# Swapped products first, and more of x and v loaded before the first period, in a long-convolution and MLP kernel

## The chip, the cores and the metric

The kernel runs on one core of a Trainium2 chip. The metric is the time of one execution on the device in microseconds (us).

## The reference

A long convolution by FFT, gated by x on both sides, and an MLP on its result:

```
h_filt = (max(pos_emb @ w1, 0) @ w2) * exp(-0.01 * pos)      # (12480, 128)
u      = x * v                                               # (4, 12480, 128)
y      = irfft(rfft(u, 2S) * rfft(h_filt, 2S))[:, :S]        # S = 12480
x2     = (x * y).reshape(49920, 128)
h      = x2 @ w_in                                           # (49920, 2048)
out    = (h * clip(h + 3, 0, 6) / 6) @ w_out                 # (49920, 128)
```

All in 32-bit floats.

## The kernel before, in words

The order of the instructions on each engine is that of the code. Transfers are all issued on SP's queue, in the code's order, and a transfer into a buffer waits there until the buffer's last reader is done.

The convolution is a Fourier transform in two stages each way. It comes in 8 *groups* of 32 channels and 2 batch rows. For a group: a product u = x * v on POOL (a *gate*, L453, in *halves* of 16 channels: 8 halves a group), a first stage on PE (L282, copied to the tile z by ACT, L294), a second stage (L301) that makes the spectrum, the product with the filter's spectrum h (`products`), a third stage (L546, copied by ACT, L550), then transposes (L557, copied by ACT, L560) and a fourth stage (L575, results L594 and L596).

`filter` runs first. It makes the filter's spectrum, and in its last part does group 0's first stage: 8 *visits* of 4 first-stage steps. Then come 8 *periods*, one a group. `period(g)` goes through 25 *chunks* of 4 frequencies: products of chunk c, third stage of an earlier chunk, second stage of chunk c + 1. Between chunks it does the transposes of group g - 1, the visits of group g + 1 and the decoding of the MLP's weights on DVE (`weight`, L225 to L247, and L243 on ACT). So the second stage of chunk c + 1 goes into one of two banks in PSUM (`s2`), which chunk c - 1 used, and waits until all readers of that bank are done. In `products`, ACT copies the spectrum into a bank `sw` (one buffer) with halves swapped and one negated (L499, L500, "the swap"). DVE makes four products, "the block": q and a from the spectrum's bank (L520, L521), q2 and a2 from the swapped bank (L522, L523). POOL adds them up (L527). In period 0 the last addition of two chunks in three is on DVE (L533).

x and v come in halves into the pool xv (two buffers). During the filter three more halves go into a pool ext. `gate_next` multiplies the next loaded half, and if its buffers were of xv, loads a further half into them. A list of chunks in `period` says when (GATES, and GATES0 for period 0).

After the periods the MLP runs (class Moe, from about 1000 us to the end). The change doesn't touch it.

Of the kernel before, what the change touches and what calls it, by code (L numbers as in the profile page):

```python
# [38 lines left out]
GB = 2  # L39
# [24 lines left out]
VISIT = 4  # L64
GATES = (1, 4, 8, 11, 14, 17, 20, 22)
GATES0 = (0, 2, 4, 8, 11, 14, 17, 20, 22)
NT = 8
NH = 4

# [119 lines left out]
def pool(tc, name, bufs=1, **kw):  # L189
    return tc.tile_pool(name=name, bufs=bufs, reuse_waits="tile", **kw)  # L190
# [60 lines left out]
class Conv:  # L251
# [54 lines left out]
    def filter(self, pos_emb, w1, w2, f_tab, win_d, ident_d):  # L306
        tc, nc = self.tc, self.nc
# [64 lines left out]
        def spectrum(half, c, stp):  # L372

            t, kw = self.second_stage(ftab[:, c * CH :], z, c)
            tv = t.rearrange("p (k s g c) -> p k s g c", k=CH, s=2, c=G)
            st = stp.tile([P, 2, CH, 2, G], F32, tag="st", name="st")
            sv = st.rearrange("p g k s c -> p k s g c")
            nc.scalar.copy(sv[:, :kw, 0], tv[:, :kw, 0])
            for i, op in ((0, ALU.add), (1, ALU.subtract)):
                nc.vector.tensor_tensor(out=sv[:, i:kw:2, 1], in0=tv[:, i:kw:2, 1], in1=sv[:, i:kw:2, 0], op=op)  # L380
            nc.sync.dma_start(
                self.hd[half].rearrange("g p k s c -> p g k (s c)")[:, :, c * CH : c * CH + kw],
                st[:, :, :kw].rearrange("p g k s c -> p g k (s c)"),
            )
# [12 lines left out]
            spectrum(0, c, st0)  # L397
        early.close()
        self.ext = ExitStack()
        ext = self.ext.enter_context(pool(tc, "ext", 3, side="right"))  # L400
        for piece in range(2 * GB):
            for j in range(G // 4):
                self.first_stage(z, u[:, piece], 0, piece, j)
# [2 lines left out]
        large.close()  # L406
        self.ft = self.left.enter_context(pool(tc, "ft", NT))
        st1 = large.enter_context(pool(tc, "st1", 12))
        for c in range(NCHUNK):
            spectrum(1, c, st1)  # L410
            if c % 2 and self.n_tabs < NT:
                self.load_tab()
        large.close()
        left, right = self.left, self.right
# [31 lines left out]
    def gate_next(self):  # L446

        if self.loaded:
            half, xt, vt, again = self.loaded.pop(0)
            if half == 0:  # L450
                self.gated.append(self.up.tile([R[0], G, N1], F32, tag="u", name="u"))
            u = self.gated[-1][:, half * G // 2 : (half + 1) * G // 2, :]
            self.nc.gpsimd.tensor_tensor(out=u, in0=xt, in1=vt, op=ALU.mult)  # L453
            if again:
                self.load_next()

    def visit(self, g, m):

        piece, j = divmod(m * VISIT, G // 4)
        for i in range(VISIT):  # L460
            self.first_stage(self.z[g % 2], self.gated[0], piece // GB, piece, j + i)
        if j + VISIT == G // 4:
            self.gated.pop(0)
# [39 lines left out]
    def products(self, item):  # L503

        nc, P = self.nc, 128
        g, c, kw, t, tab = item
        sw = self.swapped(t, kw)
        hs = self.hs.pop(0)
        a = self.pr.tile([P, CH, 2 * GB, G], F32, tag="a", name="pa", bufs=4)
        a2 = self.pr.tile([P, CH, 2 * GB, G], F32, tag="a2", name="pa2")  # L510
        q = self.pr.tile([P, CH, GB, G], F32, tag="q", name="pq")
        q2 = self.pr.tile([P, CH, GB, G], F32, tag="q2", name="pq2")
        uv = t.rearrange("p (k s g) -> p k s g", k=CH, g=G)[:, :kw]
        sv = sw.rearrange("p (k s g) -> p k s g", k=CH, g=G)[:, :kw]

        def h(ci, si, m):
            return hs[:, ci, :kw, si, :].unsqueeze(2).to_broadcast([P, kw, m, G])

        mul, add = ALU.mult, ALU.add
        nc.vector.tensor_tensor(out=q[:, :kw], in0=uv[:, :, :GB], in1=h(0, 1, GB), op=mul)  # L520
        nc.vector.tensor_tensor(out=a[:, :kw], in0=uv, in1=h(0, 0, 2 * GB), op=mul)  # L521
        nc.vector.tensor_tensor(out=q2[:, :kw], in0=sv[:, :, :GB], in1=h(1, 1, GB), op=mul)  # L522
        nc.vector.tensor_tensor(out=a2[:, :kw], in0=sv, in1=h(1, 0, 2 * GB), op=mul)  # L523
        self.load_h()

        def plus(x, y):
            nc.gpsimd.tensor_tensor(out=x, in0=x, in1=y, op=add)  # L527

        plus(a[:, :kw, GB:], q[:, :kw])
        plus(a2[:, :kw, GB:], q2[:, :kw])  # L530
        if self.sum:
            s, s2 = self.sum
            nc.vector.tensor_tensor(out=s, in0=s, in1=s2, op=add)  # L533
        self.sum = None
        if g == 0 and c % 3:
            self.sum = a[:, :kw], a2[:, :kw]
        else:
            plus(a[:, :kw], a2[:, :kw])
        return g, c, kw, tab, a
# [61 lines left out]
    def period(self, g):  # L601


        n = 0
        if g == 1:
            self.ext.close()
            self.dp = self.left.enter_context(pool(self.tc, "dp"))
            self.wp = self.right.enter_context(pool(self.tc, "wp", 2, side="right"))
        for c in range(NCHUNK):
            end = min(32, 32 * (c + 1 - START) // (NCHUNK - 1 - START))  # L610
            self.chunk(g, c)
            if c in (0, NCHUNK - 1):
                self.fourth_stage()
            if c in (GATES if g else GATES0):
                self.gate_next()
            while n < end:
                if g:
                    self.back(g - 1, 4 * n)
                    self.weight(n)
                n += 1  # L620
                if n % VISIT == 0:
                    if g + 1 < NG:
                        self.visit(g + 1, n // VISIT - 1)
                    if n < 28 and g + 1 < NG:
                        self.fourth_stage()
                if n % VISIT == 2 and VISIT < n < 28 and g + 1 == NG:
                    self.fourth_stage()
# [267 lines left out]
```

## Time and profile before

| | |
|---|---|
| time, median of 3 runs | 3170.02 us (3169.38 to 3170.16) |
| the profiled execution: time | 3166.51 us |
| its span, first to last instruction | 3164.7 us |
| PE, ACT, DVE, POOL busy in the span | 98%, 74%, 73%, 66% |
| granted TensorE clock, mean | 0.998 |
| moved by DMA | 304.66 MB |
| waits of L301 for L521 | 27.9 us, 21 times |

A row of the order of time has the start in us from the span's start, the length in us, the engine, the line, the operation, the tiles (out<-in, numbers left out, so that the banks s2, sw and s3 may read s, sw and s), how many instructions were merged, and in brackets how long the engine was idle before and what ended that. PE is TensorE, DVE is VectorE, ACT is ScalarE, POOL is GpSimd. The filter runs until 158 us, period 0 to about 242, and the other periods take some 111 us each. In this text chunk k's L301 is the second stage that makes chunk k's spectrum, and block k its four products.

### The profile page before, as it was taken

To read this page: it belongs to the slowest core of one execution; us is meant where nothing else is said; L and a number is where in the kernel's file an instruction comes from. 1 tells how busy PE (TensorE), PEld (TensorE's weight loads), DVE (VectorE), ACT (ScalarE), POOL (GpSimd) and SP (SyncE) were. 2 spreads that over 40 slices of the span, in tenths; PEclk is the share of its full clock that TensorE was granted. 3 is DMA by queue.
4 is the path that set the end of the run, shared out by engine and by line. 5 is a ranking of instruction groups with operands and counts; after the bars stand their busy time and mean duration, and the time that the engine had idled before them with its cause. 6 is when DMAs were issued, how large, how long until landed. Compare 5 with 4: busy or idle time off the path is not lost.

```text
span 3164.7 us, 53332 instructions
## 1 busy us (share of the span) xinstructions
PE 3114.2 (98%) x19916; PEld 2633.9 (83%) x19916; DVE 2305.8 (73%) x2707; ACT 2351.7 (74%) x3039; POOL 2079.2 (66%) x1240
## 2 busy tenths in 40 slices
PE   9989999999999999999999999999999999999999
PEld 8978888888887788888888888888888888888887
DVE  4467666767654777777777777777777777777776
ACT  2367767767766777878787777777777877777777
POOL 1188777777874666666666666666666666666666
PEclk9999999999999999999999999999999999999999
DMA  6688888787855111111111110111111111111110
GB/s 236 211 205 230 228 230 234 218 238 221 228 172 202 54 36 35 38 42 35 35 40 31 41 41 30 41 39 32 41 36 35 39 32 41 38 33 40 40 31 24
DMA packets 232273, 304.66 MB, mean 96 GB/s; under 512 B 38055, under 2 KB 159310, under 8 KB 231118
## 3 DMA queue, kind: packets, MB, share of 16 engines
q1 hardware_dynamic: 232014, 301.26, 32.6%
q8 instruction: 157, 2.57, 0.3%
q14 instruction: 102, 0.84, 0.1%
HBM read 224.87 MB, written 76.28 MB: 95 GB/s over the span
## 4 chain that ended last, share of the span: by engine, by line
PE 68%; POOL 0%; DVE 0%; ACT 0%; DMA 0%; issue 0%; ACTq 0%
PE acc L827 11%; PE acc L823 11%; PE acc L824 11%; PE ph L788 11%; PE ph L790 11%; PE ph L789 11%; PE ts L575 0%; PE s L557 0%; PE ts L557 0%; POOL pa L527 0%; DMA yd<-y 0%; POOL glo L812 0%; DVE y L596 0%; ACT o L594 0%; ACT ghi L810 0%
## 5 line engine op out<-in xcount | busy, mean ns | idle before, releaser
L812 POOL TENSOR_TENSOR glo<-g,ghi 128x1024 fp32r<-128x1024 f32 x588 | 1404.4, 2397 | 761.2 <-ACT ghi L810 761.0
L800 DVE SCALAR_TENSOR_TENSOR g<-r,ph 128x1024 f32<-128x1024 f32 (+1 forms) x784 | 949.7, 1211 | 408.7 <-ACT r L798 408.3
L798 ACT ACTIVATE r<-ph,three 128x1024 f32<-128x1024 f32 (+1 forms) x784 | 871.1, 1111 | 273.6 <-PE ph L790 273.4
L810 ACT CAST ghi<-g 128x1024 fp32r<-128x1024 f32 (+1 forms) x784 | 811.1, 1035 | 1.9 <-DVE g L800 1.0
L788 PE MATMUL ph<-xhi,win_hi 128*128 128x512 f32 (+1 forms) x1568 | 608.5, 388 | 0.0
L789 PE MATMUL ph<-xlo,win_hi 128*128 128x512 f32 (+1 forms) x1568 | 608.4, 388 | 0.0
L790 PE MATMUL ph<-xhi,win_lo 128*128 128x512 f32 (+1 forms) x1568 | 608.3, 388 | 0.0
L824 PE MATMUL acc<-ghi,wout_lo 128*128 128x512 f32 (+1 forms) x1568 | 608.0, 388 | 0.0
L823 PE MATMUL acc<-ghi,wout_hi 128*128 128x512 f32 (+1 forms) x1568 | 607.9, 388 | 0.0
L827 PE MATMUL acc<-glo,wout_hi 128*128 128x512 f32 (+1 forms) x1568 | 481.3, 388 | 0.6 <-POOL glo L812 0.6
L527 POOL TENSOR_TENSOR pa<-pa,pq 128x256 f32<-128x256 f32 (+1 forms) x400 | 295.6, 747 | 171.3 <-DVE pa L521 133.2
L788 PEld LDWEIGHTS ph<-xhi,win_hi 128*128 128x128 f32 x1568 | 294.4, 188 | 61.5 <-issue 0.8
L827 PEld LDWEIGHTS acc<-glo,wout_hi 128*128 128x128 f32 x1568 | 293.6, 188 | 61.7 <-POOL glo L812 1.5
L824 PEld LDWEIGHTS acc<-ghi,wout_lo 128*128 128x128 f32 x1568 | 294.5, 188 | 60.5
L790 PEld LDWEIGHTS ph<-xhi,win_lo 128*128 128x128 f32 x1568 | 294.4, 188 | 60.5
L823 PEld LDWEIGHTS acc<-ghi,wout_hi 128*128 128x128 f32 x1568 | 294.4, 188 | 60.4
L789 PEld LDWEIGHTS ph<-xlo,win_hi 128*128 128x128 f32 x1568 | 294.5, 188 | 60.4
L812 DVE TENSOR_TENSOR glo<-g,ghi 128x1024 fp32r<-128x1024 f32 x196 | 283.7, 1448 | 0.0
L520 DVE TENSOR_TENSOR pq<-s,h 128x256 f32<-128x256 f32 (+1 forms) x200 | 84.1, 421 | 255.7 <-POOL pa L527 162.2
L761 DVE TENSOR_TENSOR xy<-xt,yt 128x512 f32<-128x512 f32 x96 | 258.7, 2695 | 0.0
L301 PE MATMUL s<-z,tab 128*128 128x128 f32 x1584 | 213.9, 278 | 35.5 <-DVE pa L521 27.9
L527 POOL TENSOR_TENSOR pa<-pa,pa 128x512 f32<-128x512 f32 (+1 forms) x184 | 232.5, 1263 | 14.4
(61 smaller groups left out, 3620.6 us busy)
## 6 DMA issues: line engine op xcount, KB each, us to landing
tab<-in_g_tab SPq DMA_DIRECT2D x192, 256.0 KB
h<-hd SPq DMA_DIRECT2D x384, 128.0 KB
yd<-y SPq DMA_DIRECT2D x64, 512.0 KB
xt<-in_xt SPq DMA_DIRECT2D x98, 256.0 KB
out<-o SPq DMA_DIRECT2D x97, 256.0 KB
xt<-in_x SPq DMA_DIRECT2D x64, 384.0 KB
vt<-in_v SPq DMA_DIRECT2D x64, 384.0 KB
yt<-yd SPq DMA_DIRECT2D x256, 64.0 KB
```

Of the source, the lines that this page charges most:

```text
L527: nc.gpsimd.tensor_tensor(out=x, in0=x, in1=y, op=add)
L761: self.nc.vector.tensor_tensor(out=xy.rearrange("p (n e c) -> p n e c", e=4, c=GH), in0=xt.rearrange("p (n e c) -> p n e c", e=4, c=GH), i ...
L788: nc.tensor.matmul(ph[:, i, :ne], self.win_hi[:, sl], hi[:, :ne], start=True, stop=False)
L789: nc.tensor.matmul(ph[:, i, :ne], self.win_hi[:, sl], lo[:, :ne], start=False, stop=False)
L790: nc.tensor.matmul(ph[:, i, :ne], self.win_lo[:, sl], hi[:, :ne], start=False, stop=True)
L798: nc.scalar.activation(r[:, :, :ne], ph[:, :, :ne], AF.Relu, bias=self.three)
L800: nc.vector.scalar_tensor_tensor(out=g[:, :, :ne], in0=r[:, :, :ne], scalar=6.0, in1=ph[:, :, :ne], op0=ALU.min, op1=ALU.mult)
L810: nc.scalar.copy(ghi[:, :, :ne], g[:, :, :ne])
L812: e.tensor_tensor(out=glo[:, :, :ne], in0=g[:, :, :ne], in1=ghi[:, :, :ne].bitcast(F32), op=ALU.subtract)
L823: nc.tensor.matmul(a, self.wout_hi[:, f, :], ghi[:, i, :ne], start=(f == 0), stop=False)
L824: nc.tensor.matmul(a, self.wout_lo[:, f, :], ghi[:, i, :ne], start=False, stop=False)
L827: nc.tensor.matmul(a, self.wout_hi[:, f, :], glo[:, i, :ne], start=False, stop=(f == NFC - 1))
```

## The change

Three things:

- In `products` q2 and a2, which read the swapped bank, are made before q and a, which read the spectrum's bank. POOL's additions follow in the same order.
- `gate_next`, while it runs in the filter, loads a further half also after a half of the pool ext, into ext again: three halves more are under way before period 0.
- In period 0 the visits of group 1 come at chunks 0, 2, 6, 9, 12, 15, 18 and 21. Before, they came at chunks 3, 6, 9, 12, 15, 18, 21 and 23.

```diff
+VISITS0 = (2, 6, 9, 12, 15, 18, 21)
...
-        ext = self.ext.enter_context(pool(tc, "ext", 3, side="right"))
+        ext = self.spare = self.ext.enter_context(pool(tc, "ext", 3, side="right"))
...
             if again:
                 self.load_next()
+            elif self.ps is None:
+                self.load_next(self.spare)
...
+        nc.vector.tensor_tensor(out=q2[:, :kw], in0=sv[:, :, :GB], in1=h(1, 1, GB), op=mul)
+        nc.vector.tensor_tensor(out=a2[:, :kw], in0=sv, in1=h(1, 0, 2 * GB), op=mul)
         nc.vector.tensor_tensor(out=q[:, :kw], in0=uv[:, :, :GB], in1=h(0, 1, GB), op=mul)
         nc.vector.tensor_tensor(out=a[:, :kw], in0=uv, in1=h(0, 0, 2 * GB), op=mul)
-        nc.vector.tensor_tensor(out=q2[:, :kw], in0=sv[:, :, :GB], in1=h(1, 1, GB), op=mul)
-        nc.vector.tensor_tensor(out=a2[:, :kw], in0=sv, in1=h(1, 0, 2 * GB), op=mul)
...
+        plus(a2[:, :kw, GB:], q2[:, :kw])
         plus(a[:, :kw, GB:], q[:, :kw])
-        plus(a2[:, :kw, GB:], q2[:, :kw])
...
             end = min(32, 32 * (c + 1 - START) // (NCHUNK - 1 - START))
+            if g == 0:
+                end = VISIT * (1 + sum(c >= i for i in VISITS0))
```

Line numbers of the changed kernel are a little higher: L520 to L523 are L525, L526, L523 and L524 there, L301 is L302, L282 is L283, L442 is L443, L484 is L487, L546 is L549.

DVE, in period 1, around a block in the weights' decoding (s2 is the spectrum's bank, sw the swapped one, h the filter's spectrum), before:

```order
L241 SCALAR_TENSOR_TENSOR dec_3596<-dec_3596 128x256
L520 TENSOR_TENSOR pq_3916<-s2_3887,h_3690 128x256
L521 TENSOR_TENSOR pa_3914<-s2_3887,h_3690 128x512
L522 TENSOR_TENSOR pq2_3917<-sw_3911,h_3690 128x256
L523 TENSOR_TENSOR pa2_3915<-sw_3911,h_3690 128x512
L245 TENSOR_TENSOR dec_3596<-dec_3596,raw_3594 128x256
```

The same place on DVE now:

```order
L242 SCALAR_TENSOR_TENSOR dec_3596<-dec_3596 128x256
L523 TENSOR_TENSOR pq2_3917<-sw_3911,h_3690 128x256
L524 TENSOR_TENSOR pa2_3915<-sw_3911,h_3690 128x512
L525 TENSOR_TENSOR pq_3916<-s2_3887,h_3690 128x256
L526 TENSOR_TENSOR pa_3914<-s2_3887,h_3690 128x512
L246 TENSOR_TENSOR dec_3596<-dec_3596,raw_3594 128x256
```

The two products of the spectrum's bank (s2_3887) moved from the block's start to its end; what stands around the block stayed.

PE at the start of period 0 (u_1819 is the last piece of group 0, u_1902 and u_1914 the first of group 1; every second stage is an L301 or L302), before:

```order
L301 MATMUL s2_1988<-z0_78,tab_1380 128x128 x4
L301 MATMUL s2_2010<-z0_78,tab_1402 128x128 x4
L301 MATMUL s2_2038<-z0_78,tab_1424 128x128 x4
L301 MATMUL s2_2060<-z0_78,tab_1446 128x128 x4
L546 MATMUL s3_2091<-pa_1996,tab_1380 128x128 x4
L301 MATMUL s2_2099<-z0_78,tab_1468 128x128 x4
L282 MATMUL ts_2104<-ctab_84,u_1902 64x99 x8
```

The same place on PE now:

```order
L302 MATMUL s2_2006<-z0_78,tab_1380 128x128 x4
L302 MATMUL s2_2028<-z0_78,tab_1402 128x128 x4
L283 MATMUL ts_2040<-ctab_84,u_1914 64x99 x8
L283 MATMUL ts_2050<-ctab_84,u_1914 64x99 x8
L283 MATMUL ts_2060<-ctab_84,u_1914 64x99 x8
L283 MATMUL ts_2070<-ctab_84,u_1914 64x99 x8
L302 MATMUL s2_2096<-z0_78,tab_1424 128x128 x4
L302 MATMUL s2_2118<-z0_78,tab_1446 128x128 x4
L283 MATMUL ts_2131<-ctab_84,u_1914 64x99 x8
```

The first visit (four first-stage steps) moved from behind chunk 4's second stage to behind chunk 1's, and the second visit to behind chunk 3's.

SP from the filter's end to the first h load of period 0 (h_1641 is the last h load of the filter; each half is two issues for x and two for v), before:

```order
L484 DMA h_1641<-hd0_57 64x2x256 x2
L442 DMA xt_1726<-in_x 96x1024
L442 DMA xt_1726<-in_x 2x1024
L442 DMA vt_1727<-in_v 96x1024
L442 DMA vt_1727<-in_v 2x1024
L442 DMA xt_1733<-in_x 96x1024
L442 DMA xt_1733<-in_x 2x1024
L442 DMA vt_1734<-in_v 96x1024
L442 DMA vt_1734<-in_v 2x1024
L484 DMA h_2004<-hd0_57 64x2x256 x2
L442 DMA xt_2016<-in_x 96x1024
```

The same place on SP now, from the second issue of the third half on:

```order
L443 DMA xt_1821<-in_x 2x1024
L443 DMA vt_1822<-in_v 96x1024
L443 DMA vt_1822<-in_v 2x1024
L443 DMA xt_1828<-in_x 96x1024
L443 DMA xt_1828<-in_x 2x1024
L443 DMA vt_1829<-in_v 96x1024
L443 DMA vt_1829<-in_v 2x1024
L443 DMA xt_1916<-in_x 96x1024
L443 DMA xt_1916<-in_x 2x1024
L443 DMA vt_1917<-in_v 96x1024
L443 DMA vt_1917<-in_v 2x1024
L487 DMA h_2022<-hd0_57 64x2x256 x2
```

Three halves (xt_1821, xt_1828 and xt_1916, with their v), twelve issues, moved ahead of the first h load.

## The prediction, made before the changed kernel was run

> **What bounds the kernel now.** I read the page's engine shares first, then the waits, then busy time by stretch, then the order of time on PE, ACT and DVE inside one period. From the page, and from the list of waits (total, times, longest, in us):
>
> ```profile
> PE 3114.2 (98%) x19916; PEld 2633.9 (83%) x19916; DVE 2305.8 (73%) x2707; ACT 2351.7 (74%) x3039; POOL 2079.2 (66%) x1240
> ...
> ACT sw L499 <- DVE pa L523: 97.3, 85, 2.6
> POOL u L453 <- DMA vt<-in_v: 39.9, 2, 35.6
> PE s L301 <- DVE pa L521: 27.9, 21, 2.1
> ```
>
> PE is busy 98% of the span, so a gain can only come out of some 50 us of idle PE; whatever makes PE wait costs in full, since it works through its matmuls in order. Its largest wait is that of the second stage (L301) for the product L521, which frees a spectrum bank. ACT's copies into the swapped bank (L499) wait longer in sum, but ACT has room.
>
> Busy time by stretch: us, PE, PEld, DVE, ACT, POOL, clock, DMA share, GB/s.
>
> ```profile
> 158.00:170.00 12.00, 7.62 (x48) 7.21 (x48) 6.89 (x14) 3.81 (x7) 7.54 (x8) 0.86 0.20 58
> 190.60:200.90 10.30, 8.91 (x113) 8.36 (x112) 7.26 (x15) 6.65 (x14) 8.63 (x9) 1.00 0.89 217
> 335.00:339.00 4.00, 3.86 (x36) 3.61 (x38) 3.93 (x7) 2.41 (x5) 3.76 (x4) 0.67 0.58 163
> ```
>
> Period 0 begins at 158 with idle DMAs and goes on in cycles of three chunks, 10.30 us each, in which no engine is full. Later periods are PE's.
>
> **The change: products of the swapped spectrum first.** No instruction is added. In a DVE block of four products, L520 and L521 read the spectrum bank (two of them), L522 and L523 the swapped bank (one). Now the swapped bank comes free two products earlier and the spectrum bank two later. The block starts when the swap is done in either order, as these rows of period 3 show (chunk 4's end to chunk 7's L301):
>
> ```profile
> 485.07 0.84 PE L557 MATMUL ts<-ident,z 128*99 128x128 f32 x4
> 488.21 1.06 PE L546 MATMUL s<-pa,tab 128*128 128x128 f32 x8
> 489.10 1.11 PE L301 MATMUL s<-z,tab 128*128 128x128 f32 x8
> 485.94 0.59 ACT L560 COPY w<-ts 99x512 f32<-99x512 f32 x1 [0.98 <-PE ts L557]
> 486.56 0.56 ACT L499 COPY sw<-s 64x512 f32<-64x512 f32 x1
> 487.14 0.57 ACT L500 ACTIVATE sw<-s 64x512 f32<-64x512 f32 x1
> 487.80 0.42 DVE L520 TENSOR_TENSOR pq<-s,h 128x256 f32<-128x256 f32 x1 [1.33 <-POOL pa L527]
> 488.14 0.68 DVE L521 TENSOR_TENSOR pa<-s,h 128x512 f32<-128x512 f32 x1
> 489.07 0.68 DVE L523 TENSOR_TENSOR pa<-sw,h 128x512 f32<-128x512 f32 x1
> ```
>
> The swap at 486.56 follows ACT's copy L560, which follows PE's L557; the swap ends at 487.71, the block starts 0.09 later. The releaser named for L520 (POOL) is not the last one: the swap is. L521 ends at 488.82, and L301 of chunk 7, which takes the bank that L521 frees, starts 0.28 later, 0.89 after L546: PE is just not late. With the new order the product that frees this bank ends where L523 ends now, 489.75, which is 0.93 later; L301 starts at about 490.03, and PE idles 0.93. The earlier swapped bank can't move this block forward, since its swap waits for PE through L560, not for the bank.
>
> How often is L301 that close? The same period's other pairs, in the order chunk 4 (PE waits already), 10, 16, 19, 21, 22, 24; each L301 with the L521 two blocks before:
>
> ```profile
> 476.16 1.13 PE L301 MATMUL s<-z,tab 128*128 128x128 f32 x8 [0.71 <-DVE pa L521]
> 501.72 0.68 DVE L521 TENSOR_TENSOR pa<-s,h 128x512 f32<-128x512 f32 x1
> 502.71 1.06 PE L301 MATMUL s<-z,tab 128*128 128x128 f32 x8
> 528.33 0.68 DVE L521 TENSOR_TENSOR pa<-s,h 128x512 f32<-128x512 f32 x1
> 529.11 1.13 PE L301 MATMUL s<-z,tab 128*128 128x128 f32 x8 [0.47 <-ACT raw L243]
> 541.11 0.68 DVE L521 TENSOR_TENSOR pa<-s,h 128x512 f32<-128x512 f32 x1
> 542.07 1.06 PE L301 MATMUL s<-z,tab 128*128 128x128 f32 x8
> 551.52 0.68 DVE L521 TENSOR_TENSOR pa<-s,h 128x512 f32<-128x512 f32 x1
> 552.48 1.06 PE L301 MATMUL s<-z,tab 128*128 128x128 f32 x8
> 557.16 1.13 PE L301 MATMUL s<-z,tab 128*128 128x128 f32 x8 [2.06 <-DVE pa L521]
> 566.71 0.68 DVE L521 TENSOR_TENSOR pa<-s,h 128x512 f32<-128x512 f32 x1
> 567.49 0.91 PE L301 MATMUL s<-z,tab 128*128 128x128 f32 x6
> ```
>
> The rooms are 0.31, 0.10, 0.28, 0.28 and 0.10 us, all under 0.93. Chunks 21 and 22 count once: 22's block is held by the weight decoding on DVE, so that a PE made late at 21 waits less there. That makes seven points with chunk 7. I count four (4, 7, 16, 19) in full, 4 x 0.93 = 3.7, and three (10, 22, 24) at half, 3 x 0.47 = 1.4, because in these DVE's own backlog, which doesn't shift with PE, sets part of the block's start. That is 5.1 us a period. Ends: 0, if all is absorbed, and 7 x 0.93 = 6.5. Periods 1 to 6 have this pattern: 6 x 5.1 = +30.6. Period 7 has no first-stage visits, so fewer tight points; I take half, +2.5, between 0 and 6.5.
>
> **Period 0.** One cycle of it, from a visit's chunk to the next:
>
> ```profile
> 199.85 1.13 PE L301 MATMUL s<-z,tab 128*128 128x128 f32 x8 [1.39 <-DVE pa L521]
> 206.89 0.68 DVE L523 TENSOR_TENSOR pa<-sw,h 128x512 f32<-128x512 f32 x1
> 207.68 0.56 ACT L499 COPY sw<-s 64x512 f32<-64x512 f32 x1 [1.59 <-DVE pa L523]
> 209.22 0.68 DVE L521 TENSOR_TENSOR pa<-s,h 128x512 f32<-128x512 f32 x1
> 210.15 1.13 PE L301 MATMUL s<-z,tab 128*128 128x128 f32 x8 [1.39 <-DVE pa L521]
> ```
>
> Here the swap does wait for L523 (ends 207.57, swap 0.11 later). With the new order that release comes 0.93 earlier, swap and block start 0.93 earlier; but the freeing product is then last, 0.93 later in its block. It ends at 209.90 as before, and L301 starts at 210.15 as before. So the 1.39 us per cycle stay: 0 from the steady part. The adds on POOL change places with their products, 0.
>
> **First visit at chunk 0, loads earlier.** The eighth visit leaves chunk 23 and the first comes at chunk 0, where PE idles:
>
> ```profile
> 162.28 1.13 PE L301 MATMUL s<-z,tab 128*128 128x128 f32 x8 [1.66 <-DVE pa L521]
> 165.54 1.90 PE L301 MATMUL s<-z,tab 128*128 128x128 f32 x8 [2.12 <-DVE pa L521]
> ...
> 491.50 2.96 PE L282 MATMUL ts<-ctab,u 98*64 98x99 f32 x64
> 559.11 4.17 PE L282 MATMUL ts<-ctab,u 97*64 97x99 f32 x64
> ...
> 162.98 1.23 SPq L484 DMA_DIRECT2D h<-hd  x2
> 174.72 0.42 DVE L520 TENSOR_TENSOR pq<-s,h 128x256 f32<-128x256 f32 x1 [1.19 <-ACT sw L500]
> ...
> xt<-in_x SPq DMA_DIRECT2D x64, 384.0 KB
> ```
>
> A visit is 3 us of PE (the row at 491.50). It fills these 3.8 us of idleness, but its four copies on ACT stand ahead of the next swap, so the chain of swaps and blocks gets longer at the start by about as much as it gets shorter at the end. I take -1.5, between -3.8 (both gaps gone) and +3 (a whole visit in the chain). Three halves more are 3 x 2 x 384 KB = 2.3 MB, at 217 GB/s some 11 us of transfer, moved into the time before 170 where the DMAs are nearly idle. No POOL product of period 0 waits for its half (the 39.9 us above are two waits, 35.6 of them one), so the earlier arrival earns 0. On SP's queue the twelve extra issues stand ahead of the first h load of period 0, which goes out when block 0 ends (162.98) for block 4 (174.72): 11 us of traffic begun near 155 ends before it is needed. If that cover were gone, block 4 would be late by a few us, once.
>
> **Clock.** The row 335:339 shows a granted clock of 0.67 just after a gap of 2 us like that at 557.16, and the visit after that one takes 4.17 us against 2.96: 1.2 us. The new gaps may bring one such stretch to more periods; I take +1, between 0 and 14 (six periods, two stretches each). The Trainium skill ("TensorE: Matmul & The Clock Gate", section "Part 1: The HAM clock gate") says that the clock halves after at least one idle window of about 3.4 us. By that rule no gap here is long enough and the term is 0; the row of 335:339 speaks against it, with a far shorter gap.
>
> **Sum.** +30.6 + 2.5 - 1.5 + 1 = +32.6. The profiled run took 3166.5 us (span 3164.7), 3.5 under the median; it becomes 3199, and the median 3170.0 becomes 3202.6. I say 3202.
>
> **Rivals.**
> Faster: the swapped bank is the bottleneck in the tight chunks too. The wait list supports it, 97.3 us in 85 of 200 swaps. If the tight blocks' swaps waited for L523, their blocks would start 0.93 earlier, L301 would lose nothing, and perhaps half of its 27.9 us would go: 3170 - 14 = 3156. It decides at the moment where the swap of chunk 5 starts before the copy L560 of chunk 4 ends; the row at 486.56 says it can't. Chance 0.10.
> No change: half the loss (2.5 a period, 17 in all) is regained, because period 0's DMA share of 0.89 and more hides a limit that the moved loads lift, by up to their 11 us, and both idle gaps at the start go (3.8): 3172. Against it: no wait there names a DMA. Chance 0.07.
> Deeper: all points in full and the clock falls twice in each period: 6 x 6.5 + 6.5 + 14 = +59, at most 3229; halfway, 3218. Chance 0.09.
> The forecast itself has 0.74. Its own range, from half the loss (+15) to all points in full with a few clock stretches (+45), is 3185 to 3215. To leave out no more than two in ten I go to 3174 and 3218. A change under 0.2% (6 us) can't be told from none here. Slower 0.83, the same 0.07, faster 0.10.
>
> **What would show it.** Right: the waits of L301 for the last product of the block grow from 27.9 us to 55 or more, chunk 7's start to chunk 10's (489.10 to 502.71 here) takes some 0.9 us longer, ACT's waits for the swapped bank shrink, period 0 is within 4 us of its length and PE's idle time grows by some 30 us. Wrong: if L301's waits don't grow in periods 1 to 6, blocks start earlier than I hold possible; if POOL waits for a half or DVE for h, the loads collided.

## The result and the profile after

| | before | changed |
|---|---|---|
| time, median of 5 runs each | 3170.02 us (3169.18 to 3171.23) | 3205.37 us (3204.2 to 3206.46) |
| span of the profiled execution | 3164.7 us | 3203.6 us |

The changed kernel is slower: the ratio is 1.0111, with a 95% interval of 1.0097 to 1.0126. The forecast was 3202.

The page's engine line of the changed kernel, then three rows of its list of waits (total us, times, longest), then the group of second-stage matmuls (busy, mean ns | idle before them, and what ended it) in the changed kernel:

```profile
PE 3118.3 (97%) x19916; PEld 2632.2 (82%) x19916; DVE 2310.8 (72%) x2707; ACT 2366.2 (74%) x3039; POOL 2080.4 (65%) x1240
...
PE s L302 <- ACT sw L502: 34.4, 38, 2.7
ACT sw L502 <- DVE pa L524: 22.5, 29, 1.4
PE s L302 <- DVE pa L526: 17.5, 14, 2.2
...
L302 PE MATMUL s<-z,tab 128*128 128x128 f32 x1584 | 216.4, 280 | 69.4 <-ACT sw L502 34.4 <-DVE pa L526 17.5 <-DMA yd<-y 8.2
```

and the same group before:

```profile
L301 PE MATMUL s<-z,tab 128*128 128x128 f32 x1584 | 213.9, 278 | 35.5 <-DVE pa L521 27.9 <-issue 3.5 <-ACT raw L243 2.3
```

PE's work is the same; its idle time ahead of the second stage went from 35.5 to 69.4 us, +33.9, and that is the change. ACT's waits for the swapped bank fell from 97.3 us (85 times) to 22.5 (29 times): that bank does come free earlier, and nothing is won by it here.

Where those microseconds lie, from the starts of the L301 (L302) in the two traces. Period 0 runs from its first second stage to that of chunk 1 in period 1, periods 1 to 6 from there to the same place one period on, period 7 to the last second stage:

| us | before | changed | difference |
|---|---|---|---|
| filter, up to the first second stage of period 0 | 158.60 | 162.24 | +3.6 |
| period 0 | 87.76 | 88.37 | +0.6 |
| periods 1 to 6 together | 661.12 | 691.96 | +30.8 |
| period 7 | 78.09 | 82.88 | +4.8 |
| from there to the end | 2179.1 | 2178.1 | -1.0 |

The first row isn't the change: it ends at 158.6 to 163.2 in the profiles of kernels whose filter is the same code as before's, and this before stands at the early end of that. This fits its profiled execution, which was 3.5 us under its median.

Period 3 around chunk 7 in the changed kernel, in order of time on PE, ACT and DVE. These rows answer to those of 485 to 490 before (L560 is the transpose, L563 ACT's copy of it, L549 the third stage, L502 and L503 the swap, L523 and L524 the swapped bank's products, L525 and L526 the spectrum's):

```profile
500.10 0.84 PE L560 MATMUL ts<-ident,z 128*99 128x128 f32 x4
503.24 1.06 PE L549 MATMUL s<-pa,tab 128*128 128x128 f32 x8
505.04 1.13 PE L302 MATMUL s<-z,tab 128*128 128x128 f32 x8 [0.75 <-DVE dec L226]
500.97 0.59 ACT L563 COPY w<-ts 99x512 f32<-99x512 f32 x1 [0.99 <-PE ts L560]
501.58 0.56 ACT L502 COPY sw<-s 64x512 f32<-64x512 f32 x1
502.18 0.57 ACT L503 ACTIVATE sw<-s 64x512 f32<-64x512 f32 x1
502.83 0.42 DVE L523 TENSOR_TENSOR pq<-sw,h 128x256 f32<-128x256 f32 x1 [1.33 <-POOL pa L530]
503.17 0.68 DVE L524 TENSOR_TENSOR pa<-sw,h 128x512 f32<-128x512 f32 x1
504.10 0.68 DVE L526 TENSOR_TENSOR pa<-s,h 128x512 f32<-128x512 f32 x1
```

The swap still follows ACT's copy of PE's transpose; the block still begins 0.08 after the swap (502.75); L526 ends at 504.78 and L302 starts at 505.04, 0.26 later. Before, PE did not stop here; now it stops for 0.75 us and starts 0.91 later. The releaser in brackets is a decoding instruction that began as L526 ended: two events close together, and the profile names the other one. That holds for the other names too. Set against the ends of L526 in the whole trace, all 73 waits of L302 over 0.15 us, 68.7 us together, end 0.10 to 0.35 us after the L526 two blocks before, whatever is named; before, the same is true of L521 for 34.1 us. So the waits for the spectrum's bank doubled. Chunks 10, 16 and 19 as examples:

```profile
518.30 0.68 DVE L526 TENSOR_TENSOR pa<-s,h 128x512 f32<-128x512 f32 x1
519.09 1.13 PE L302 MATMUL s<-z,tab 128*128 128x128 f32 x8 [0.25 <-issue]
545.90 0.68 DVE L526 TENSOR_TENSOR pa<-s,h 128x512 f32<-128x512 f32 x1
546.68 1.13 PE L302 MATMUL s<-z,tab 128*128 128x128 f32 x8 [1.46 <-ACT sw L502]
559.61 0.68 DVE L526 TENSOR_TENSOR pa<-s,h 128x512 f32<-128x512 f32 x1
560.39 1.13 PE L302 MATMUL s<-z,tab 128*128 128x128 f32 x8 [0.59 <-ACT sw L502]
```

In these three the second stage starts 0.10 to 0.11 us after the end of L526.

Period 0, one cycle of it in the changed kernel, and two stretches (us, PE, PEld, DVE, ACT, POOL, clock, DMA share, GB/s):

```profile
191.50 1.13 PE L302 MATMUL s<-z,tab 128*128 128x128 f32 x8 [0.92 <-ACT sw L502]
193.98 1.13 PE L302 MATMUL s<-z,tab 128*128 128x128 f32 x8 [0.46 <-DVE pa L526]
201.78 1.13 PE L302 MATMUL s<-z,tab 128*128 128x128 f32 x8 [0.92 <-ACT sw L502]
...
161.64:173.64 12.00, 8.69 (x134) 8.20 (x136) 6.83 (x14) 5.84 (x12) 7.44 (x8) 1.00 0.92 237
190.60:200.90 10.30, 8.91 (x112) 8.35 (x112) 8.02 (x15) 6.88 (x14) 8.69 (x9) 1.00 0.57 167
```

The cycle is 10.28 us long (10.30 before), and its 1.39 us of idle PE is now two waits of 0.92 and 0.46. The first stretch begins 0.60 us before the period's first second stage, as the one from 158 to 170 does before. The early visit is there (PE busy 8.69 of 12 us, before 7.62), and so are the early loads (DMA share 0.92 for 0.20, and 0.57 for 0.89 later on), yet the period isn't shorter.

### The profile page after: what moved, and what is told of

Its sections match the earlier page's. It is cut to its first block, busy times and chain, and to the rows that moved or that the text cites. A ratio compares the mean times of both kernels' runs of the same rounds, so it can differ in the third digit from the quotient of the medians.

```text
span 3203.6 us, 53407 instructions
## 1 busy us (share of the span) xinstructions
PE 3118.3 (97%) x19916; PEld 2632.2 (82%) x19916; DVE 2310.8 (72%) x2707; ACT 2366.2 (74%) x3039; POOL 2080.4 (65%) x1240
## 4 chain that ended last, share of the span: by engine, by line
PE 72%; ACT 1%; DVE 0%; DMA 0%; POOL 0%; issue 0%; SPq 0%; DVEq 0%; ACTq 0%; POOLq 0%
PE acc L832 11%; PE acc L829 11%; PE acc L828 11%; PE ph L795 11%; PE ph L794 11%; PE ph L793 11%; PE ts L560 2%; PE ts L578 1%; PE s L302 1%; PE s L549 1%; PE ts L283 1%; PE s L560 0%; DMA yd<-y 0%; ACT w L563 0%; ACT sw L502 0%
## 5 line engine op out<-in xcount | busy, mean ns | idle before, releaser
L523 DVE TENSOR_TENSOR pq<-sw,h 128x256 f32<-128x256 f32 (+1 forms) x200 | 83.8, 419 | 283.4 <-POOL pa L530 147.6
L302 PE MATMUL s<-z,tab 128*128 128x128 f32 x1584 | 216.4, 280 | 69.4 <-ACT sw L502 34.4
L302 PEld LDWEIGHTS s<-z,tab 128*128 128x128 f32 x1584 | 193.3, 192 | 82.0 <-ACT sw L502 76.2
```

Source lines behind the costliest of these rows:

```text
L302: self.nc.tensor.matmul(t[:, i * 128 : (i + 1) * 128], tab[:, i, :], z[:, c * CH + i, :], start=True, stop=True)
```

## Experiments

Kernels made from the one before keep its line numbers, and there L520 to L523 are the four products in the order in which that kernel makes them. So the product a, the last reader of the spectrum's bank, is L521 in the old order, L523 in the change's order and L522 in the half step.

**The parts apart.** One kernel is the kernel before with the new order of products and additions, and nothing else of the change; another has the early loads and the early visit, and the old order.

> The products and additions in the new order; loads and visits as before. Theory (the spectrum's bank comes free at the block's end, 0.93 us later, and PE's second stage waits for it some seven times a period): the whole loss, +33 to +38 us, 3203 to 3208; idle time of PE ahead of the second stage grows from 35.5 us to about 70. Rival A (the loss comes from the loads or from the visits of period 0): within 5 us of before, 3165 to 3175.

> The early loads and the new visits of period 0; the products in the old order. Theory: -4 to +1 us against before, 3166 to 3171, all of it between the start of period 0 and the start of period 1. Rival A (the loads or visits cost): +30 us or more.

Measured: the order alone 3206.67 us, ratio 1.0117 (1.0102 to 1.0133), the whole loss. The loads and the visit alone 3169.96 us, ratio 1.0001 (0.9992 to 1.0009), nothing. By stage, the order alone has the changed kernel's periods 1 to 6 and its period 7 to 0.1 us (691.94 and 82.87 us), and the other one has the old ones to 0.2 us (661.00 and 78.08). In period 0 the order alone adds 1.1 us and the loads and the visit alone add 1.7. The loads and the visit were not run apart from each other.

**A third bank for the spectrum.** If the loss is that the spectrum's bank comes free late, a third bank takes it away. PSUM has no bank to spare, so the third stage gives up one of its two, in both orders:

```diff
-    BANKS = {"s2": 2, "sw": 1, "s3": 2, "ts": 3}
+    BANKS = {"s2": 3, "sw": 1, "s3": 1, "ts": 3}
```

> Before, with three banks for the spectrum (s2) and one for the third stage (s3), instead of two and two. It is the control for the next. Theory: the second stage no longer waits for L521 (27.9 us now), but the third stage may wait for its one bank; between -20 and +30 us against before, 3150 to 3200.

> The same three banks and one, with the products in the new order. Theory: with a third bank the second stage of chunk c + 1 takes the bank of chunk c - 2, freed a whole chunk earlier, so the late release costs nothing: within 5 us of the control with the old order, faster by up to 10 if the early swapped bank helps. Rival B (the new order costs because the early swap disturbs ACT or DVE, whatever the banks): slower than its control by 25 to 40 us.

Measured: 3180.5 us with the old order, ratio 1.0034 (1.0021 to 1.0046), and 3160.56 with the new one, ratio 0.9974 (0.9964 to 0.9983). The order that cost 36.9 us with two banks wins 19.9 with three. The groups of the third, the second and the first stage, in the old order and then the new one:

```profile
L546 PE MATMUL s<-pa,tab 128*128 128x128 f32 x1584 | 222.0, 283 | 25.4 <-ACT z L550 22.6 <-POOL pa L527 1.7
L301 PE MATMUL s<-z,tab 128*128 128x128 f32 x1584 | 210.3, 276 | 1.5 <-DVE pa L521 0.8 <-issue 0.7
L282 PE MATMUL ts<-ctab,u 98*64 98x99 f32 (+1 forms) x5120 | 237.0, 249 | 16.6 <-ACT w L560 13.8 <-ACT z L294 2.3 <-DVE u L365 0.5
```

```profile
L546 PE MATMUL s<-pa,tab 128*128 128x128 f32 x1584 | 221.4, 283 | 20.7 <-ACT z L550 17.9 <-POOL pa L527 2.3 <-DVE pq L520 0.3
L301 PE MATMUL s<-z,tab 128*128 128x128 f32 x1584 | 211.1, 277 | 5.9 <-DMA tab<-in_g_tab 2.9 <-DVE pa L523 2.3 <-issue 0.7
L282 PE MATMUL ts<-ctab,u 98*64 98x99 f32 (+1 forms) x5120 | 235.8, 250 | 2.5 <-ACT w L560 2.0 <-DVE u L365 0.5
```

The waits of the second stage are all but gone in both (68.6 us with the new order and two banks), and both pay some 20 us for the third stage's single bank. So the loss of the new order hangs on the late release of the spectrum's bank, and without it the early release of the swapped bank is worth something. It is worth more than the 10 us that were allowed for at most, and by a way that the expectation did not name. In the old order PE's first stage (L282) waits 13.8 us for L560, ACT's copy of the transposes, which empties a bank that this stage needs. L560 stands behind the swap in ACT's order, and the swap waits for the block. In the new order that wait is 2.0 us, and this difference is the largest part of the 19.9.

**Half a step, and another way to be late.** In one kernel only the short product of the swapped bank goes first, so that the spectrum's bank comes free 0.34 us later instead of 0.93. In another the block begins with the spectrum's bank, but also ends with it:

```diff
 before         q,  a,  q2, a2
+half a step    q2, q,  a,  a2
+begins and ends with the spectrum's bank:  q, q2, a2, a
```

> The kernel before, with the block of four products in the order q2, q, a, a2: only one product of the swapped bank, the short one, stands ahead of the two of the spectrum's bank, so that bank comes free about 0.34 us later than before (L520 at 487.80 to L521 at 488.14 in period 3) instead of 0.93 later, and the swapped bank comes free last, as before. Theory (PE pays the late release of the spectrum's bank, less the room that each place has): the rooms in period 3 are 0.31, 0.10, 0.28, 0.28, 0.10 and none at chunks 4 and 21, so a delay of 0.34 leaves about 0.34 + 0.03 + 0.24 + 0.06 + 0.06 + 0.24, some 1.0 a period with half of the last ones absorbed to 1.5 in full, 7 to 11 us in all: 3177 to 3181. Rival (PE pays for beginning the block with the swapped bank, since the block's first product then waits for the swap): the whole 35, 3205. Rival (only a delay past some point counts): 3170.

> The kernel before, with the order q, q2, a2, a, and POOL's addition for the swapped bank first: the block still begins with a product of the spectrum's bank, but the last reader of that bank is last in the block, as in the change; the swapped bank comes free 0.68 earlier than before. Theory (the late release of the spectrum's bank): about the whole loss of the reordered kernel alone, 3200 to 3208, with L301's waits near 69 us. Rival (what costs is that the block begins with the swapped bank's products): no loss, 3165 to 3175.

Measured: the half step 3197.72 us, ratio 1.0077 (1.0063 to 1.0091), 26 us where 7 to 11 were expected: a miss of the theory and of both rivals. The other 3215.59 us, ratio 1.0139 (1.0125 to 1.0153): the loss doesn't hang on what the block begins with, but it is 44 us, more than the change's 37 and above the 3200 to 3208 expected. The half step's trace, first PE at chunks 4 and 10 of period 3:

```profile
490.94 1.13 PE L301 MATMUL s<-z,tab 128*128 128x128 f32 x8 [1.05 <-DVE pa L522]
...
519.59 1.13 PE L301 MATMUL s<-z,tab 128*128 128x128 f32 x8 [1.55 <-issue]
```

At chunk 4 the wait grew from 0.71 to 1.05, by the 0.34 of the release. At chunk 10, where PE did not wait before, it waits 1.55. The block that it waits for stands behind the decoding on DVE. Here is how that decoding begins, on DVE and POOL, first before, then in the half step:

```profile
489.67 0.28 DVE L225 TENSOR_SCALAR dec<-raw 128x256 int32<-128x256 int32 x1
487.40 2.37 POOL L453 TENSOR_TENSOR u<-xt,vt 98x1024 f32<-98x1024 f32 x1
489.73 1.56 POOL L527 TENSOR_TENSOR pa<-pa,pq 128x256 f32<-128x256 f32 x2
```

```profile
504.47 1.77 DVE L225 TENSOR_SCALAR dec<-raw 128x256 int32<-128x256 int32 x1
502.35 2.37 POOL L453 TENSOR_TENSOR u<-xt,vt 98x1024 f32<-98x1024 f32 x1
504.67 1.43 POOL L527 TENSOR_TENSOR pa<-pa,pq 128x256 f32<-128x256 f32 x2
```

Before, L225 started 0.10 us ahead of the end of POOL's gate (489.77), took 0.28 and ended 0.18 behind that end, before POOL's next additions were through. In the half step it started 0.25 ahead, and its 1.77 us reach to 0.14 after the end of POOL's next two additions (506.10). Over all periods the group of L225, before, in the order alone, in the half step and in the kernel that ends with the spectrum's bank:

```profile
L225 DVE TENSOR_SCALAR dec<-raw 128x256 int32<-128x256 int32 x16 | 14.8, 926 | 0.0
```

```profile
L225 DVE TENSOR_SCALAR dec<-raw 128x256 int32<-128x256 int32 x16 | 16.3, 1020 | 0.0
```

```profile
L225 DVE TENSOR_SCALAR dec<-raw 128x256 int32<-128x256 int32 x16 | 25.4, 1586 | 0.0
```

```profile
L225 DVE TENSOR_SCALAR dec<-raw 128x256 int32<-128x256 int32 x16 | 24.7, 1542 | 0.0
```

All eleven decoding instructions on DVE together took 122.0, 122.1, 136.5 and 136.4 us in these four. So the two that came out dearer than expected are those in which DVE loses that race, and the change itself is not one of them. The Trainium skill ("SBUF — State Buffer", section "Who interferes with whom") says that DVE and GpSimd share a pair of ports under an exclusive lock for certain DVE instructions, and that the loser is blocked for a whole instruction. These rows fit that, with 1.77 us in place of 0.28, but here L225 was held until three POOL instructions were through, and no run shows by itself that it is one of those instructions.

A part of the half step's miss has nothing to do with decoding: its period 0, in which nothing is decoded, took 91.8 us instead of 87.8. Its cycle of three chunks is 10.63 us long instead of 10.30. The expectation had counted tight places alone.

**Without the decoding.** To see the release by itself, the decoding's eleven DVE instructions are left out in three kernels (old order, half step, the change's order).

```diff
-    ts(out=ai, in0=high, scalar1=0x7FFFFFFF, scalar2=None, op0=ALU.bitwise_and)
...
-    nc.scalar.activation(hi.bitcast(F32R), a, AF.Copy)
+    nc.scalar.activation(hi.bitcast(F32R), hi.bitcast(I32), AF.Copy)
...
-    nc.vector.tensor_tensor(out=lo.bitcast(F32R), in0=a, in1=s, op=ALU.add)
+    nc.scalar.activation(lo.bitcast(F32R), lo.bitcast(I32), AF.Copy)
```

> The kernel before without the decoding of the weights on DVE: its eleven instructions (L225 to L241, L245, L247) are left out, and ACT writes the two halves of a weight from the raw words instead (two instructions, where there was one), so the MLP computes with other numbers at the same cost. It is the control for the two kernels below. What it does against the kernel before is expected from the traces alone: the gap at chunk 22 (2.06 to 2.24 us a period), which the decoding holds, goes, -6 to -14 in all: 3156 to 3164.

> The order q2, q, a, a2 without the weights' decoding (left out as in its control). With the decoding this order cost 26 us where 7 to 11 were expected: its trace shows L301 of chunks 4 and 7 late by the 0.34 and 0.32 that the release predicts, but chunk 10 by 1.75, behind decoding instructions of DVE that lasted far longer than in the kernel before (L225 1.77 us in period 3 against 0.28, each ending as a POOL instruction ends). Theory (the release costs 0.34 at each tight place, the rest is decoding held behind POOL's work): against its control +8 to +15. Rival (a later release costs more than its delay at tight places, decoding or not): +20 to +30. Rival (nothing is left without DVE's backlog): 0 to +3.

> The order q2, a2, q, a (the change's, and nothing else of it) without the weights' decoding, against the same control. Theory (PE pays the delay of the release, 0.93, less the room at each place): about as much as with the decoding, +28 to +40, and 2.3 to 3.5 times what the order q2, q, a, a2 costs here. Rival (the loss of the change, too, is mostly decoding that got later): +5 to +20, and much the same as the other order.

Measured against the kernel before: 0.9949 (0.9937 to 0.9962), 0.9994 (0.9985 to 1.0003) and 1.0068 (1.0056 to 1.0081), medians 3153.94, 3167.42 and 3190.84 us. Against their own control the half step costs 13.5 us and the change's order 36.9: both are in their ranges, and the change's order costs what it cost with the decoding. The second is 2.7 times the first, as 0.93 is 2.7 times 0.34, but that is luck. By stage, period 0 has 3.6 us of the half step's loss and 1.1 of the other's, while periods 1 to 6 have 10.1 and 35.3, 3.5 times as much. More than 2.7 is what the theory asks for, since the room of a place comes off a short delay as well as a long one. The control itself gained 16.0, a little more than its range. How much later each tight second stage of period 3 came, against the control of the same kind (chunk to chunk, from the traces; the 22 includes 21):

| chunk | share counted in the prediction | change | half step | half step, no decoding | change's order, no decoding |
|---|---|---|---|---|---|
| 4 | full 0.93 | 0.93 | 0.34 | 0.33 | 0.93 |
| 7 | full 0.93 | 0.91 | 0.32 | 0.31 | 0.91 |
| 10 | half 0.47 | 0.42 | 1.75 | 0.10 | 0.69 |
| 16 | full 0.93 | 0.99 | 0.49 | 0.16 | 0.76 |
| 19 | full 0.93 | 0.75 | 0.16 | 0.16 | 0.75 |
| 21 and 22 | half 0.47 | 1.01 | 0.49 | 0.33 | 0.68 |
| 24 | half 0.47 | 0.00 | 0.02 | 0.33 | 0.93 |
| whole period | 5.1 | 5.1 | 3.5 | 1.7 | 5.8 |

The 1.75 at chunk 10 shrank to 0.10 when the decoding went. The theory holds for the tight places, with the addition that a block behind the decoding moves by POOL's timing as well. The kernel whose block ends with the spectrum's bank was not run without decoding, so for its 44 us that part is read from the trace alone.

**The swapped bank alone, and everything together.** A second swapped bank gives the old order what the new one was to give it, without the late release (BANKS with sw 2, s3 1). The last kernel is the whole changed kernel with three spectrum banks.

> The kernel before in its old order, with two swapped banks and one bank for the third stage (BANKS sw 2, s3 1): the swap never waits for the block before, and the spectrum's bank comes free as early as in the kernel before. It is to be set against the two kernels with three spectrum banks (old order 3180.5, new order 3160.6), which also have one bank for the third stage. Theory: in the tight chunks the swap waits for PE through ACT's copies, so a free swapped bank gains nothing in periods 1 to 6 beyond what three spectrum banks show, L301's waits there stay near the 27 us of before; period 0, where the swap does wait for the block (1.39 us a cycle), gets shorter by up to 8 us; the single third-stage bank costs some us: 3165 to 3180. Rival (the swapped bank is the bottleneck in the tight chunks): L301's waits shrink by half in periods 1 to 6, 3150 to 3162.

> The whole changed kernel (new order, three more early halves, the first visit at chunk 0) with three spectrum banks and one third-stage bank. It is to be set against the reordered kernel with the same banks (3160.6), whose period 0 was held once for some 7 us behind a late table while the DMAs were full (share 1.08 and 1.01 in the two stretches from 180 to 200). Theory: with the release out of the way, DMA traffic is what bounds the start of period 0, and the loads made before 170 lift that: 3150 to 3157. Rival (the early loads and the early visit earn nothing, as they did with two spectrum banks): 3158 to 3163. Rival (the twelve extra issues on SP's queue delay the tables or h at the start): over 3163.

Measured: two swapped banks 3174.39 us, ratio 1.0008 (0.9999 to 1.0017). Periods 2 to 6 take 108.2 to 111.5 us each in it, as with the old order and three spectrum banks (108.2 to 111.6), and period 0 got 1.5 us shorter. In periods 1 to 6 the second stage still waits 12.4 us for L521, where it waited 14.5 before, and at chunk 4 of period 3 still 0.70 (0.71). So the swapped bank is not what held the tight chunks. In period 0 the waits of 1.39 us are gone from the cycle, but PE waits there for tables that come late (4.6 us).

The whole change with three banks takes 3159.74 us, ratio 0.9962 (0.9950 to 0.9975), the lowest median of those that leave nothing out. That is where the rival put it (3158 to 3163, the early loads and the visit earn nothing), and not the theory (3150 to 3157): it is 0.8 us under the reordered kernel with three banks, and their intervals overlap. Yet the traces differ in period 0, 83.4 us against 88.4. Of these 4.9 us the whole change gave back 2.2 in later stages, and its filter happened to be 2.0 longer. So in these two traces the early loads and the visit shorten period 0, and why later stages gave some of it back is open. In period 0 the reordered kernel waited once for a table, and the visit behind it ran at a lower clock:

```profile
190.66 2.05 PE L301 MATMUL s<-z,tab 128*128 128x128 f32 x8 [2.91 <-DMA tab<-in_g_tab]
192.64 4.69 PE L282 MATMUL ts<-ctab,u 98*64 98x99 f32 x64
```

Two stretches of it (columns as above), then the second of them in the whole change with three banks:

```profile
180.00:190.00 10.00, 7.10 (x86) 6.43 (x82) 8.68 (x17) 6.78 (x13) 9.36 (x11) 0.97 1.08 235
190.00:200.00 10.00, 9.05 (x91) 8.54 (x92) 2.91 (x6) 3.59 (x7) 4.53 (x4) 0.69 1.01 229
```

```profile
190.00:200.00 10.00, 9.34 (x117) 8.74 (x118) 8.43 (x16) 6.88 (x14) 8.69 (x9) 1.00 0.56 161
```

With the loads made early the DMA share there is 0.56, no table is late in this stretch, and DVE is busy 8.43 of 10 us instead of 2.91.

## Why the prediction was right, point by point

**The main term, +30.6.** Measured +30.8 over periods 1 to 6, and the mechanism is shown three ways: by the rows (L302 0.10 to 0.26 us behind L526), by a third bank, which takes the loss away and turns it round, and by the two delays without decoding. The sign that was named, waits of 55 us or more for the block's last product, is there by the ends of that product (68.7 us) and not by the releasers' names (17.5 us). That the sum came out to 0.2 is in part luck, for the parts inside a period were less exact and cancelled: chunk 24 gave 0 for 0.47, chunks 21 and 22 gave 1.01 for 0.47. Chunk 19 was counted in full and gave 0.75. It had a room of 0.28, and chunk 16 shows that 0.10 is enough from the release to the start, so 0.18 of the delay was free. Chunk 7 to chunk 10 was to take 0.9 longer and took 0.44 (505.04 to 519.09, 14.05 us for 13.61): that sentence contradicted the half weight that the sum gave chunk 10, and the half weight was right.

**Period 7, +2.5.** Measured +4.8: the mis-sized term. I took half because the period has no first-stage visits, and it is 78.1 us long, not some 111 like the others. But it has six tight places of its own (chunks 4, 9, 11, 14, 17 and 24, 0.58 to 0.91 each, 4.5 in sum). It should have been counted in the trace like period 3.

**Period 0, -1.5.** The steady cycle was right: 10.3 us, with 1.39 idle in it. The visit at the start was not worth 1.5: the period is 0.6 longer, and 1.7 longer with the old order. PE has its work at once, but the swap that follows is late by the visit's copies on ACT, and the wait comes back behind the visit:

```profile
164.20 2.95 PE L283 MATMUL ts<-ctab,u 98*64 98x99 f32 x64
...
170.94 1.13 PE L302 MATMUL s<-z,tab 128*128 128x128 f32 x8 [2.71 <-ACT sw L502]
```

**Loads 0.** Nothing speaks against it with two spectrum banks: POOL's waits for vt are 39.8 us for 39.9, no block of period 0 finds DVE idle and waits for h, and loads and visit together came to nothing (3169.96 us). No run has the loads without the visit, so that they are worth 0 and the visit costs what period 0 lost is argued, not shown. The price of the twelve issues on SP's queue did not show either.

**Clock, +1.** Wrong: there are fewer stretches of half clock before the MLP, one in the changed kernel for four, and they cost nothing. The stretch after the gap at chunk 22 before, the same place in the changed kernel, and in the loads and the visit alone:

```profile
555.00:561.00 6.00, 3.94 (x37) 3.60 (x38) 5.90 (x12) 2.73 (x6) 4.03 (x5) 0.77 0.64 200
```

```profile
576.56 1.13 PE L302 MATMUL s<-z,tab 128*128 128x128 f32 x8 [2.24 <-DVE pa L526]
...
574.00:580.00 6.00, 3.76 (x55) 3.48 (x56) 5.93 (x12) 2.84 (x7) 4.20 (x4) 1.00 0.64 210
```

```profile
560.00:566.00 6.00, 3.95 (x63) 3.78 (x64) 5.90 (x12) 3.33 (x7) 4.04 (x5) 1.00 0.63 198
...
572.48 0.91 PE L302 MATMUL s<-z,tab 128*128 128x128 f32 x6 [1.42 <-issue]
```

The gap before was 2.06 us and the clock fell; in the changed kernel it was 2.24 and the clock did not (the last section says why). Nor does a fall cost anything here: where the visit runs at full clock, PE waits 1.42 us two chunks on, at chunk 24, and where it ran slowly, before, PE did not wait there. Before, period 3 had such a fall and period 4 had none, and they took 110.93 and 110.94 us. The Trainium skill ("TensorE: Matmul & The Clock Gate", section "Part 1: The HAM clock gate") has the clock halved after an idle window of about 3.4 us. The traces here differ from that: 2.06 us of idle PE was enough before.

**The rivals.** "Faster" needed the swap to wait for the block in the tight chunks: two swapped banks show that it does not. "No change" needed a hidden DMA limit: with two spectrum banks the loads and the visit alone gained nothing, so none shows. "Deeper" took every tight place in full and twice the clock: the places came to 5.1 of 6.5. (Halfway between 3202 and 3229 would have been 3216, not 3218.)

**The sum.** +32.6 forecast and +35.4 between the medians. The stages without the filter come to 0.6 + 30.8 + 4.8 - 1.0 = +35.2: period 7 gave 2.3 more than forecast, period 0 gave 2.1 more, the clock 1 less, and the end 1.0 less. So here too misses on both sides cancel, and the total is closer than its smaller terms. The profiles differ by 38.9, of which 3.6 is the filter.

## What to carry to other kernels

Ahead of reordering the readers of two buffers, ask which buffer's release the bounding engine waits for: the readers of that one go first, and a wait with a larger sum on an engine with room is no reason to turn them round. Do not go by the name of the releaser alone: set the end of the bank's last reader against the start of its next writer. Measure the room at each place, from the end of the last reader to the start of the next writer, and count every stage in the trace, the last one too. If the better order for one buffer delays another, give the delayed one a further buffer before judging the order: here the sign changed, from +37 to -20 us.

## What the runs showed of the hardware

A DVE instruction of the decoding took 0.28 us or 1.77 us depending on whether it began 0.10 or 0.25 us ahead of the end of a POOL instruction. In five traces (before, the changed kernel, the order alone, the half step, and the kernel that ends with the spectrum's bank) L225 (L226 in the changed kernel) begins six times less than 0.3 us ahead of the end of POOL's gate. In the first three it began 0.09 to 0.15 us ahead and took 0.28 to 0.30 us, all 18 times; in the other two it began 0.17 to 0.25 us ahead and took 1.70 to 1.77 us, all 12 times. So a shift of about 0.1 us between the two engines cost some 1.4 us on DVE, and the change stood just on the cheap side.

In the trace of before, the four stretches of half clock, each 3.41 us long, begin 170.67, 221.87 and 221.87 us apart, which are 50 and 65 times 3.413: they lie on a grid. The Trainium skill ("TensorE: Matmul & The Clock Gate", section "What's actually happening") has a free-running window of 3413 ns, and the trace agrees with that.

The grid also tells why one gap of 2.06 us is caught and one of 2.24 is not. Before, the gap at chunk 22 lay whole in one window in periods 1, 3 and 5, 2.06 us each time, and half clock followed. In periods 2 and 4 the end of a window split it, into 1.43 and 0.63 to 0.66 us, and none followed. The 2.24 us in period 3 of the changed kernel were split into 1.34 and 0.90. From 150 to 920 us in the thirteen traces of this case, leaving out windows at half clock themselves, all 22 windows with 1.94 us or more of idle PE were followed by half clock, 6 of the 19 with 1.60 to 1.93, and none of the 2843 with less. What decides between 1.60 and 1.93 is open; the ends of matmuls in a trace are modelled, so the border may be no sharper than that.
